# Linear attention and a SiLU feed-forward in one kernel: sums of x, sums of W2 and the first transposes of batch 1 placed elsewhere in the order of work

## The chip, the cores and the metric

The kernel runs on one core of a Trainium2 chip. The metric is the device time of one execution in microseconds, the median of several runs.

## The reference

q, k and v have the shape 8 batches x 8 heads x 576 tokens x 64, all float32. Attention is the linear kind: a softmax of q over its 64 features, a softmax of k over the 576 tokens, then two small products. Its output, 4608 tokens by 512, is the x of a feed-forward layer with a hidden width of 2048.

```python
q_s = exp(q) / sum(exp(q), axis=-1)          # over the features
k_s = exp(k) / sum(exp(k), axis=2)           # over the tokens
kv  = einsum('bhsd,bhse->bhde', k_s, v)
x   = einsum('bhsd,bhde->bhse', q_s, kv)     # then (tokens, heads*64)
h   = x @ w_in                               # 4608 x 2048
out = (h * sigmoid(h)) @ w_out               # 4608 x 512
```

## The kernel before, in words

**Two layers of work.** A batch of attention gives 576 rows of x. The feed-forward part works on chunks of 512 tokens, nine in all. Chunk t needs the rows of batch t and some of the batch before, so batch t+1 is prepared while chunk t is multiplied.

**Preparing a batch.** q, k and v come in halves of four heads each (`load`, L97). ScalarE takes the exponential of q (`exp_q`, L108, into `eq`) and of k (`exp_k`, L113, into `ek`). The row sums of q's exponentials are taken either by VectorE alone (`qsum`, L148 to L152) or, for batch 1, by GpSimd in two pair additions (`qsum_pair`, L126 and L129, into h tiles) and then by VectorE (`qsum_end`, L136 and L137). `qnorm` (L157) multiplies `eq` by the reciprocal sums, on GpSimd or VectorE. v is cast into `vaug` (`vcast`, L91 or L89). Normalised q is transposed into `qT`: for later batches by a DMA transpose (L167), for batches 0 and 1 by TensorE (`tr`, L175, nine small transposes for a half) with copies out of PSUM (`trcopy`). `kv_both` multiplies k and v (L189) and scales the result (L200, L202, `kvn`); `xt` multiplies it with `qT` (L228) and copies x, transposed, into `XTS` (XT in the profile), half on VectorE and half on ScalarE.

**The two matrix products.** Both large products use a scheme that does a two-by-two block product with seven block products instead of eight, at the price of sums of the blocks. For x @ w_in the products are `group` (L368), with sums of W1's blocks in WS (`ws_op`, L319) and sums of x's blocks in XS (`xs_op`, L329), both on VectorE. XS2 is made from XS1, and XS4 from XS2. The order of the seven is 1, 2, 6, 5, 7, 4, 3; product 6 reads XS2. The results are copied (`group_snap`, L89, ScalarE or VectorE), added (`group_add`, L346, VectorE) and put through SiLU (`group_silu`, L352, ScalarE). For the product with w_out the block products are `prod` (L467), with sums of the hidden values in S (`s_op`, L441) and four sums of W2's blocks T1 to T4 (`t_op`, L451). T2 needs T1, T4 needs T2. T3 is written over a block of W2 itself (`T3 = B12`); T1 and the plain product of chunk 0 read that block before. The results leave over `snap` (L483) and `w_add` (L487) into `ow` and `store` (L401).

**The start is different.** The first 576 tokens go through `wide` (L258) with a tanh form of SiLU (L250, L251), chunk 0's second product is plain (`mm2_plain`, L405), and `mm2_plain_out` (L417 on ScalarE, L419 on VectorE) writes its four 128-row tiles. Eight units of chunk 1 are plain as well (`mm1`, L276 and L287).

**The order of the work is written by hand.** The program keeps a list of units, each some TensorE work, and for every unit a list of pieces that are emitted just before it (`plan(u, f)`). Every engine takes its instructions in the order of emission. Pieces of one unit are emitted in the order of the `plan` calls. Units 0 to 15 are `wide`; `b1 = begin[1] = 16` starts nine plain units of chunk 0's second product; units 25 to 38 interleave its rest with seven groups of chunk 1; 39 to 46 are the eight plain units of chunk 1; `begin[2] = 47` starts chunk 2, where groups of chunk 2 and products of chunk 1 take turns ("ggbgbgbgbbgbgb", g for a group, b for half a product). The sums of x of chunk t are planned at `begin[t]`. The pieces that bear on this case are these:

```python
plan(b1, lambda: (tr(1, 0, 0, 5, 6), tr(1, 0, 5, J, 7)))
...
plan(b1 + 22, lambda: t_op(1, nc.vector))
...
plan(b1 + 30, lambda: t_op(3, nc.vector))
```

**Queues of transfers.** GpSimd issues the weights and the first batches' loads, up to batch 2; SyncE's queue holds the stores and all later loads, in order of emission. Tiles of q, k and v exist twice each (`ld`, bufs=2), so a load waits until the exponential or cast of the tile two loads earlier is done.

Of the kernel before, what the change touches and what calls it, by code (L numbers as in the profile page):

```python
# [8 lines left out]
FP32 = mybir.dt.float32  # L9
BF16 = mybir.dt.bfloat16  # L10
FP16 = mybir.dt.float16
ACT = mybir.ActivationFunctionType
# [5 lines left out]
def kernel(  # L18
# [9 lines left out]
    nc = tc.nc  # L28
    B, H, S, D = q.shape
    DM, DFF = w_in.shape  # L30
    NT = B * S
    P = 64
    J = S // P
# [10 lines left out]
    OS = 0.5 / XS  # L44
# [9 lines left out]
    mp = ctx.enter_context(tc.tile_pool(name="mp", bufs=2))  # L54
# [19 lines left out]
    PS = ps.tile([128, 8, 512], FP32, name="PS")  # L74
# [10 lines left out]
    st = [dict() for _ in range(B)]  # L85

    def copy(eng, o, i):
        if eng is nc.scalar:
            eng.copy(out=o, in_=i)  # L89
        else:  # L90
            eng.tensor_copy(o, i)  # L91

    def load(b, name, src, cc, eng):
        t = ld.tile([128, 2, J * D], FP32, name=name)
        st[b][name, cc] = t
        x = src[b].rearrange("(g r) (p j) d -> g (r p) (j d)", r=2, j=J)
        eng.dma_start(out=t, in_=x.rearrange("g x y -> x g y")[:, 2 * cc:2 * cc + 2, :])  # L97

    def jgd(b, name, cc):
        return st[b][name, cc].rearrange("p g (j d) -> p j g d", d=D)  # L100

    def half(t, cc):
        return t[:, :, cc * 128:(cc + 1) * 128].rearrange("p j (g d) -> p j g d", d=D)

    def exp_q(b, cc, g0=0, g1=2):
        if "eq" not in st[b]:
            st[b]["eq"] = ap.tile([128, J, NG * D], BF16, name="eq")
        nc.scalar.activation(  # L108
            out=half(st[b]["eq"], cc)[:, :, g0:g1], in_=jgd(b, "qt", cc)[:, :, g0:g1], func=ACT.Exp
        )  # L110

    def exp_k(b, cc):
        nc.scalar.activation(out=half(ek, cc), in_=jgd(b, "kt", cc), func=ACT.Exp)  # L113
# [6 lines left out]
    def qsum_pair(b, cc):  # L120
        e = half(st[b]["eq"], cc)
        t1 = mp.tile([128, 2 * TCH], FP32, name="h0", bufs=1)[:, 0:J * D]
        t1 = t1.rearrange("p (j g d) -> p j g d", g=2, d=D // 2)
        t2 = mp.tile([128, 2 * TCH], FP32, name=f"h{cc + 1}", bufs=1)[:, 0:J * D // 2]
        t2 = t2.rearrange("p (j g d) -> p j g d", g=2, d=D // 4)
        nc.gpsimd.tensor_tensor(  # L126
            out=t1, in0=e[:, :, :, 0:D // 2], in1=e[:, :, :, D // 2:D], op=ALU.add
        )
        nc.gpsimd.tensor_tensor(  # L129
            out=t2, in0=t1[:, :, :, 0:D // 4], in1=t1[:, :, :, D // 4:D // 2], op=ALU.add  # L130
        )
        st[b]["t2", cc] = t2

    def qsum_end(b, cc):
        new_zq(b)
        nc.vector.reduce_sum(out=st[b]["zq"][:, cc], in_=st[b]["t2", cc], axis=AX.X)  # L136
        nc.vector.reciprocal(out=st[b]["rzq"][:, cc], in_=st[b]["zq"][:, cc])  # L137

    def new_zq(b):
        if "zq" not in st[b]:  # L140
            st[b]["zq"] = ap.tile([128, 2, J, 2], FP32, name="zq", bufs=2)
            st[b]["rzq"] = ap.tile([128, 2, J, 2], FP32, name="rzq", bufs=2)
# [11 lines left out]
    def qnorm(b, cc, eng):  # L154
        e = half(st[b]["eq"], cc)
        r = st[b]["rzq"][:, cc]
        eng.tensor_tensor(  # L157
            out=e, in0=e, in1=r[:, :, :, None].to_broadcast([128, J, 2, D]), op=ALU.mult
        )

    def new_qt(b):
        if "qT" not in st[b]:
            st[b]["qT"] = ap.tile([128, J, 2, 128], BF16, name="qT", bufs=2)
        return st[b]["qT"]
# [7 lines left out]
    def tr(b, cc, j0, j1, bank):  # L172
        t = PS[:, bank, :].bitcast(BF16)
        for j in range(j0, j1):
            nc.tensor.transpose(  # L175
                out=t[:, (j - j0) * 128:(j - j0 + 1) * 128],
                in_=st[b]["eq"][:, j, cc * 128:(cc + 1) * 128],
                identity=ident,
            )

    def trcopy(b, cc, j0, j1, bank, eng=nc.vector):
        t = PS[:, bank, :].bitcast(BF16)[:, 0:(j1 - j0) * 128].rearrange("x (j y) -> x j y", y=128)
        copy(eng, new_qt(b)[:, j0:j1, cc, :], t)
# [127 lines left out]
    def ws_op(i, g):  # L311
        w, f0, f1 = WS[g], 4 * g + 8, 4 * g
        in0, in1, op = {
            1: (wa(0, f1), wa(1, f1), ALU.add),
            2: (w[0], wa(0, f0), ALU.subtract),
            3: (wa(0, f0), wa(0, f1), ALU.subtract),
            4: (wa(1, f0), w[1], ALU.subtract),
        }[i]
        nc.vector.tensor_tensor(out=w[i - 1], in0=in0, in1=in1, op=op)  # L319
# [30 lines left out]
    def group_silu(t, i, f, n):  # L350
        x = group_bank(t, False) if i is None else four(t, i)
        nc.scalar.activation(out=group_out(t, f, n), in_=x, func=ACT.Silu, scale=1.0 / XS)  # L352
# [42 lines left out]
    def rows(t, col):  # L395
        b, c = divmod(t * TCH + col, S)
        return out[b * S:(b + 1) * S, :].rearrange("(p j) o -> j p o", j=J)[c // P]

    def store(t, col, o):
        for i in range(2):  # L400
            nc.sync.dma_start(out=rows(t, col + i * P), in_=o[i * P:(i + 1) * P, :])  # L401
# [8 lines left out]
                stop=(fc == NFB - 1),  # L410
            )

    def mm2_plain_out(t, ms):
        ow = mp.tile([128, 2, DM], FP32, name="ow", bufs=3)
        for i, m in enumerate(ms):
            if i == 0:
                nc.scalar.activation(out=ow[:, i], in_=PS[:, 2 + m], func=ACT.Copy, scale=OS)  # L417
            else:
                nc.vector.tensor_scalar_mul(out=ow[:, i], in0=PS[:, 2 + m], scalar1=OS)  # L419
            store(t, m * 128, ow[:, i])  # L420

# [19 lines left out]
    def t_op(i, eng, f0=0, f1=HF):  # L443
        o, in0, in1 = {
            1: (T1, B12, B11),
            2: (T2, B22, T1),
            3: (T3, B22, B12),
            4: (T4, B21, T2),
        }[i]
        f = slice(f0, f1)  # L450
        eng.tensor_tensor(out=o[:, f], in0=in0[:, f], in1=in1[:, f], op=ALU.subtract)  # L451
# [97 lines left out]
    def load_w2(f0, f1):  # L549
        nc.gpsimd.dma_start(  # L550
            out=W2[:, f0:f1, :],
            in_=w_out[f0 * 128:f1 * 128, :].rearrange("(fc p) o -> p fc o", p=128),
        )
# [58 lines left out]
    def plan(u, f):  # L612
        at.setdefault(u, []).append(f)
# [7 lines left out]
    begin = {1: len(units)}  # L621
# [133 lines left out]
    for i in (1, 2, 6, 5, 7, 4, 3):  # L755
# [3 lines left out]

    b1 = begin[1]  # L760

    plan(9, lambda: (load_w2(8, 12), exp_q(1, 0, 0, 1)))
    plan(10, lambda: (exp_q(1, 0, 1, 2), qsum_pair(1, 0)))
    plan(10, lambda: load(2, "qt", q, 0, nc.gpsimd))
    plan(12, lambda: (exp_q(1, 1, 0, 1), qsum_end(1, 0), qnorm(1, 0, nc.gpsimd)))
    plan(13, lambda: (exp_q(1, 1, 1, 2), qsum_pair(1, 1)))
    plan(14, lambda: load(2, "qt", q, 1, nc.gpsimd))
    plan(b1 + 1, lambda: exp_k(1, 0))
    plan(b1 + 2, lambda: exp_k(1, 1))
    plan(b1, lambda: (tr(1, 0, 0, 5, 6), tr(1, 0, 5, J, 7)))  # L770
    plan(b1, lambda: (trcopy(1, 0, 0, 5, 6, nc.scalar), trcopy(1, 0, 5, J, 7)))
    plan(b1, lambda: (qsum_end(1, 1), qnorm(1, 1, nc.vector)))
    plan(b1, lambda: load_w2(12, 16))
    plan(b1, lambda: nc.gpsimd.tensor_copy(GTS[1][:, :, 0:64], GTS[0][:, :, TCH:S]))
# [19 lines left out]
    plan(b1 + 17, lambda: exp_k(2, 1))  # L794
    plan(b1 + 17, lambda: (vcast(2, 0, nc.gpsimd), vcast(2, 1, nc.gpsimd)))
    plan(b1 + 22, lambda: (group_silu(1, 2, 4, 1), group_silu(1, 0, 12, 0)))
    plan(b1 + 22, lambda: t_op(1, nc.vector))
    plan(b1 + 23, lambda: mm2_plain_out(0, (0, 1)))
    plan(b1 + 24, lambda: group_silu(1, 1, 12, 1))
    plan(b1 + 24, lambda: (ws_op(1, 0), ws_op(2, 0)))  # L800
    plan(b1 + 24, lambda: [load(3, x, y, i, nc.sync) for x, y, i in (
        ("vt", v, 0), ("vt", v, 1), ("qt", q, 0), ("kt", k, 1), ("kt", k, 0), ("qt", q, 1)
    )])
    plan(b1 + 25, lambda: kv_both(2))
    plan(b1 + 26, lambda: t_op(2, nc.vector))
# [1 line left out]
    plan(b1 + 28, lambda: t_op(4, nc.vector))  # L807
    plan(b1 + 29, lambda: xt(2, 1))
    plan(b1 + 29, lambda: (ws_op(3, 0), ws_op(4, 0)))
    plan(b1 + 30, lambda: mm2_plain_out(0, (2, 3)))  # L810
    plan(b1 + 30, lambda: t_op(3, nc.vector))

    for u, f in enumerate(units):
        for g in at.get(u, ()):
# [33 lines left out]
```

The softmax here doesn't subtract the row's maximum and nothing guards it: scores larger than these inputs give would overflow.

## Time and profile before

The kernel takes 265.26 us (three runs, 264.96 to 265.47). The profiled span is 263.3 us.

| engine | busy, us | share of the span |
|---|---|---|
| TensorE, matmuls | 253.0 | 96% |
| TensorE, weight loads | 203.4 | 77% |
| VectorE | 208.6 | 79% |
| ScalarE | 186.7 | 71% |
| GpSimd | 66.3 | 25% |

The longest single waits of TensorE after the first microseconds of the kernel are these: 0.52 us at 32.5 us, where the first transposes of batch 1 wait for GpSimd's normalising, and 1.82 us at 67.7 us, where product 6 of chunk 2 waits for a sum of x. In the profile, PE is TensorE, PEld its weight loads, DVE VectorE, ACT ScalarE, POOL GpSimd and SP SyncE; a q after the name is the engine's sequencer. A timeline line gives the start in us, the duration in us, the engine, the line in the code, the operation, what it writes and reads with shapes, and how many were merged; the idle time before it and what ended it stand in brackets. W in a line that starts with L451 is T3, which lies in W2.

### The profile page before, as it was taken

How to read it: one execution, taken by the hardware profiler on the slowest of the kernel's cores; microseconds unless marked ns; L12 is line 12 of the kernel's file. 1: busy time of each engine (PE TensorE's matmuls, PEld its weight loads, DVE VectorE, ACT ScalarE, POOL GpSimd, SP SyncE). 2: the span in 40 equal slices, each digit the busy share in tenths (PEclk: the TensorE clock that was granted, in tenths of full speed). 3: DMA queues.
4: the chain of work that ended last, by engine and by line, in shares of the span. 5: the costliest groups of instructions: out<-in, count | busy, mean ns of one | idle time of the engine just before them, and what ended most of it. 6: DMA issues, size and time to landing. Idle time of an engine off the chain costs nothing.

```text
span 263.3 us, 6409 instructions
## 1 busy us (share of the span) xinstructions
PE 253.0 (96%) x2732; PEld 203.4 (77%) x2732; DVE 208.6 (79%) x268; ACT 186.7 (71%) x211; POOL 66.3 (25%) x63
## 2 busy tenths in 40 slices
PE   8899899999799999999999999999999999999993
PEld 3457645656688888888888888888888888888882
DVE  2867787679997999799979997999798448855932
ACT  5767875897696699669966996699664757574610
POOL 1753891632141305130513050305000000000004
PEclk9999999999999999999999999999999999999998
DMA  7999999679997489748974889650415002400534
GB/s 240 336 199 331 260 323 334 239 143 298 364 320 159 158 190 308 142 157 166 330 137 168 192 295 119 192 127 0 92 42 120 2 0 57 105 2 1 116 85 120
DMA packets 35452, 45.89 MB, mean 174 GB/s; under 512 B 16208, under 2 KB 19984, under 8 KB 35424
## 3 DMA queue, kind: packets, MB, share of 16 engines
q1 hardware_dynamic: 29488, 33.63, 47.2%
q0 software_dynamic: 5616, 11.60, 16.9%
q8 instruction: 21, 0.34, 0.5%
q10 hardware_dynamic: 320, 0.26, 0.3%
q14 instruction: 7, 0.06, 0.1%
HBM read 36.70 MB, written 9.44 MB: 175 GB/s over the span
## 4 chain that ended last, share of the span: by engine, by line
PE 77%; DVE 14%; POOL 2%; ACT 2%; issue 2%; DMA 1%; POOLq 0%; DVEq 0%; ACTq 0%
PE PS L467 33%; PE PS L368 31%; PE PS L405 5%; PE PS L258 3%; PE PS L228 2%; DVE zq L148 2%; DVE h L346 2%; PE PS L189 2%; DMA qt<-in_q_dram 1%; DVE T L451 1%; DVE eq L157 1%; DVE WS L319 1%; DVE S L441 1%; DVE GT L441 1%; DVE XS L329 1%
## 5 line engine op out<-in xcount | busy, mean ns | idle before, releaser
L346 DVE TENSOR_TENSOR h<-PS,h 128x1024 f32<-128x1024 f32 (+1 forms) x45 | 54.0, 1200 | 13.7 <-PE PS L368 7.8
L467 PEld LDWEIGHTS <-GT 128*128 128x128 f16 x512 | 49.6, 98 | 6.9 <-issue 1.2
L368 PEld LDWEIGHTS <-WS 128*128 128x128 f16 x480 | 46.8, 98 | 8.7 <-DVE XS L329 2.1
L467 PE MATMUL PS<-W,GT 128*128 128x256 f16 x384 | 49.1, 273 | 0.0
L368 PE MATMUL PS<-XS,WS 128*128 128x256 f16 (+1 forms) x360 | 46.3, 272 | 1.9 <-DVE XS L329 1.8
L352 ACT ACTIVATE GT<-h 128x1024 f16<-128x1024 f32 (+1 forms) x45 | 46.1, 1047 | 0.3 <-DVE h L346 0.3
L89 ACT COPY h<-PS 128x1024 f32<-128x1024 f32 (+1 forms) x35 | 35.1, 1003 | 12.9 <-PE PS L368 12.5
L157 POOL TENSOR_TENSOR eq<-eq,rzq 128x1152 bf16<-128x1152 bf16 x13 | 27.5, 2117 | 62.1 <-DVE rzq L152 61.8
L467 PEld LDWEIGHTS <-S 128*128 128x128 f16 x384 | 37.1, 98 | 5.4 <-issue 1.0
L368 PEld LDWEIGHTS <-W 128*128 128x128 f16 x360 | 34.7, 98 | 4.9 <-issue 0.5
L467 PE MATMUL PS<-T,S 128*128 128x256 f16 x256 | 32.7, 273 | 0.0
L368 PE MATMUL PS<-XT,W 128*128 128x256 f16 (+1 forms) x240 | 29.5, 272 | 0.1
L352 ACT ACTIVATE GT<-PS 128x1024 f16<-128x1024 f32 (+1 forms) x15 | 15.3, 1017 | 18.9 <-PE PS L368 18.9
L91 POOL CAST vaug<-vt 128x1152 bf16<-128x1152 f32 x12 | 13.9, 1166 | 42.6 <-DMA vt<-in_v_dram 42.6
L729 POOL DMA_DIRECT2D out_dram<-ow x5 | 2.7, 547 | 72.1 <-DVE ow L714 72.1
L108 ACT ACTIVATE eq<-qt 128x1152 bf16<-128x1152 f32 (+1 forms) x18 | 19.0, 1058 | 2.6 <-DMA qt<-in_q_dram 2.5
L113 ACT ACTIVATE ek<-kt 128x1152 bf16<-128x1152 f32 x16 | 18.4, 1154 | 1.3 <-DMA kt<-in_k_dram 1.3
L148 DVE TENSOR_REDUCE zq<-eq 128x18 f32<-128x1152 bf16 x12 | 16.1, 1345 | 3.9 <-ACT eq L108 3.9
L258 PE MATMUL PS<-XT,W 128*128 128x288 f16 x128 | 16.3, 286 | 0.5 <-DVE XT L91 0.2
L467 PE MATMUL PS<-W,S 128*128 128x256 f16 x128 | 16.5, 273 | 0.0
L487 DVE SCALAR_TENSOR_TENSOR ow<-PS,sc 128x512 f32<-128x512 f32 x7 | 4.8, 691 | 14.4 <-ACT sc L483 14.4
L258 PEld LDWEIGHTS <-W 128*128 128x128 f16 x128 | 12.4, 98 | 4.3 <-issue 1.3
(78 smaller groups left out, 348.4 us busy)
## 6 DMA issues: line engine op xcount, KB each, us to landing
out_dram<-ow SPq DMA_DIRECT2D x64, 128.0 KB, 2.4
qt<-in_q_dram SPq DMA_DIRECT2D x12, 576.0 KB, 5.0
kt<-in_k_dram SPq DMA_DIRECT2D x12, 576.0 KB, 5.5
vt<-in_v_dram SPq DMA_DIRECT2D x12, 576.0 KB, 5.2
qt<-in_q_dram POOLq DMA_DIRECT2D x4, 576.0 KB, 12.5
kt<-in_k_dram POOLq DMA_DIRECT2D x4, 576.0 KB, 12.4
vt<-in_v_dram POOLq DMA_DIRECT2D x4, 576.0 KB, 12.6
W<-in_moe_w_out_dram POOLq DMA_DIRECT2D x4, 512.0 KB, 15.4
```

The costliest lines, as they stand in the source:

```text
L89: eng.copy(out=o, in_=i)
L91: eng.tensor_copy(o, i)
L108: nc.scalar.activation(out=half(st[b]["eq"], cc)[:, :, g0:g1], in_=jgd(b, "qt", cc)[:, :, g0:g1], func=ACT.Exp)
L113: nc.scalar.activation(out=half(ek, cc), in_=jgd(b, "kt", cc), func=ACT.Exp)
L148: nc.vector.reduce_sum(out=z, in_=e, axis=AX.X)
L157: eng.tensor_tensor(out=e, in0=e, in1=r[:, :, :, None].to_broadcast([128, J, 2, D]), op=ALU.mult)
L258: nc.tensor.matmul(out=PS[:, 2 * (fb % 3) + n, 0:S // 2], lhsT=W1[:, c, fb * 128:(fb + 1) * 128], rhs=XTS[0][:, c, n * (S // 2):(n + 1) * ...
L346: nc.vector.tensor_tensor(out=four(t, i), in0=group_bank(t, True), in1=four(t, i), op=ALU.add)
L352: nc.scalar.activation(out=group_out(t, f, n), in_=x, func=ACT.Silu, scale=1.0 / XS)
L368: nc.tensor.matmul(out=PS[:, bank + p // 2, (p % 2) * HT:(p % 2) * HT + width(t)], lhsT=a[:, c, p * 128:(p + 1) * 128], rhs=bb[:, c, 0:wid ...
L405: nc.tensor.matmul(out=PS[:, 2 + tb, :], lhsT=GTS[t % 2][:, fc, tb * 128:(tb + 1) * 128], rhs=W2[:, fc, :], start=(fc == 0), stop=(fc == N ...
L467: nc.tensor.matmul(out=PS[:, bank, m * HN:(m + 1) * HN], lhsT=a[:, fc, m * 128:(m + 1) * 128], rhs=bb[:, fc, :], start=(first and fc == 0) ...
```

## The change

Three things are moved, and a few pieces around them.

- **T3 behind the sums of x of chunk 2.** `t_op(3)` goes from unit 46 to unit 48, so VectorE meets XS1 to XS4 first.
- **T1 into chunk 1.** `t_op(1)` goes from unit 38 to unit 34, between two additions of chunk 1's groups.
- **The first transposes of batch 1 one unit on**, from ahead of unit 16 to ahead of unit 17, with their copies; both exponentials of k of batch 1 are put behind them.

With these, the exponential of q, half 0, of batch 1 becomes one instruction in place of two, with its pair sums one unit earlier; batch 2's first load of q goes from unit 10 to unit 12, behind GpSimd's normalising of batch 1's half 0; `mm2_plain_out` takes one tile per call, and the load of batch 3's q half 0 and k half 1 are put between the stores of chunk 0's first two tiles, ahead of v. The purpose is that no product waits for a sum that could have been made before, and that loads come in the order of their need.

```diff
-    def mm2_plain_out(t, ms):
-        ow = mp.tile([128, 2, DM], FP32, name="ow", bufs=3)
-        for i, m in enumerate(ms):
...
+    def mm2_plain_out(t, m, eng):
+        if m % 2 == 0:
+            st[t]["ow"] = mp.tile([128, 2, DM], FP32, name="ow", bufs=3)
+        o = st[t]["ow"][:, m % 2]
...
-    plan(9, lambda: (load_w2(8, 12), exp_q(1, 0, 0, 1)))
-    plan(10, lambda: (exp_q(1, 0, 1, 2), qsum_pair(1, 0)))
-    plan(10, lambda: load(2, "qt", q, 0, nc.gpsimd))
+    plan(9, lambda: (load_w2(8, 12), exp_q(1, 0), qsum_pair(1, 0)))
     plan(12, lambda: (exp_q(1, 1, 0, 1), qsum_end(1, 0), qnorm(1, 0, nc.gpsimd)))
+    plan(12, lambda: load(2, "qt", q, 0, nc.gpsimd))
     plan(13, lambda: (exp_q(1, 1, 1, 2), qsum_pair(1, 1)))
     plan(14, lambda: load(2, "qt", q, 1, nc.gpsimd))
-    plan(b1 + 1, lambda: exp_k(1, 0))
-    plan(b1 + 2, lambda: exp_k(1, 1))
-    plan(b1, lambda: (tr(1, 0, 0, 5, 6), tr(1, 0, 5, J, 7)))
-    plan(b1, lambda: (trcopy(1, 0, 0, 5, 6, nc.scalar), trcopy(1, 0, 5, J, 7)))
+    plan(b1 + 2, lambda: (exp_k(1, 0), exp_k(1, 1)))
+    plan(b1 + 1, lambda: (tr(1, 0, 0, 5, 6), tr(1, 0, 5, J, 7)))
+    plan(b1 + 1, lambda: (trcopy(1, 0, 0, 5, 6, nc.scalar), trcopy(1, 0, 5, J, 7)))
     plan(b1, lambda: (qsum_end(1, 1), qnorm(1, 1, nc.vector)))
...
-    plan(b1 + 22, lambda: t_op(1, nc.vector))
-    plan(b1 + 23, lambda: mm2_plain_out(0, (0, 1)))
+    plan(b1 + 18, lambda: t_op(1, nc.vector))
+    plan(b1 + 23, lambda: mm2_plain_out(0, 0, nc.scalar))
+    plan(b1 + 23, lambda: (load(3, "qt", q, 0, nc.sync), load(3, "kt", k, 1, nc.sync)))
+    plan(b1 + 23, lambda: mm2_plain_out(0, 1, nc.vector))
...
     plan(b1 + 24, lambda: [load(3, x, y, i, nc.sync) for x, y, i in (
-        ("vt", v, 0), ("vt", v, 1), ("qt", q, 0), ("kt", k, 1), ("kt", k, 0), ("qt", q, 1)
+        ("vt", v, 0), ("vt", v, 1), ("kt", k, 0), ("qt", q, 1)
     )])
...
-    plan(b1 + 30, lambda: mm2_plain_out(0, (2, 3)))
-    plan(b1 + 30, lambda: t_op(3, nc.vector))
+    plan(b1 + 30, lambda: mm2_plain_out(0, 2, nc.scalar))
+    plan(b1 + 30, lambda: mm2_plain_out(0, 3, nc.vector))
+    plan(begin[2] + 1, lambda: t_op(3, nc.vector))
```

More of the change, by code (lines that the diff above doesn't have):

```diff
@@ L411, in mm2_plain @@
             )
-    def mm2_plain_out(t, ms):
-        ow = mp.tile([128, 2, DM], FP32, name="ow", bufs=3)
-        for i, m in enumerate(ms):
[L416 to L420, printed above, removed]
+    def mm2_plain_out(t, m, eng):
+        if m % 2 == 0:
+            st[t]["ow"] = mp.tile([128, 2, DM], FP32, name="ow", bufs=3)
+        o = st[t]["ow"][:, m % 2]
+        if eng is nc.scalar:
+            nc.scalar.activation(out=o, in_=PS[:, 2 + m], func=ACT.Copy, scale=OS)
+        else:
+            nc.vector.tensor_scalar_mul(out=o, in0=PS[:, 2 + m], scalar1=OS)
+        store(t, m * 128, o)
     WG = [dict() for _ in range(NCH)]
```

## The prediction

> **What bounds the kernel now.** I read first the busy line of each engine and the chain that ended last, then the engines' busy time by stretches, then the waits and the timeline of the two stretches that the edits touch.
>
> ```profile
> PE 253.0 (96%) x2732; PEld 203.4 (77%) x2732; DVE 208.6 (79%) x268; ACT 186.7 (71%) x211; POOL 66.3 (25%) x63
> ...
> PE 77%; DVE 14%; POOL 2%; ACT 2%; issue 2%; DMA 1%; POOLq 0%; DVEq 0%; ACTq 0%
> ```
>
> TensorE carries the end, and 14% of the chain runs over VectorE. The stretches say where (the first column after the time is the length, then TensorE's busy time, the weight loads', VectorE's):
>
> ```profile
> 54.13:68.22 14.09, 11.91 (x153) 7.10 (x152) 13.92 (x20) 9.68 (x17) 3.19 (x3) 1.00 0.96 272
> 68.22:83.00 14.78, 14.74 (x198) 12.61 (x197) 14.57 (x18) 14.36 (x15) 4.24 (x2) 1.00 0.87 276
> ```
>
> From 54 to 83 us VectorE never rests; from 54 to 68 TensorE loses 2.2 us, and from 68 to 83 both are full. After 83 us the chain is TensorE alone. So microseconds that TensorE gains before 83 us should come off the end one for one. The hole and what makes it (idle time before an instruction stands in brackets):
>
> ```profile
> 54.13 1.09 DVE L346 TENSOR_TENSOR h<-PS,h 128x896 f32<-128x896 f32 x1 [2.09 <-PE PS L368]
> 55.14 1.22 DVE L451 TENSOR_TENSOR T<-W 128x2048 f16<-128x2048 f16 x1
> ...
> 63.57 1.16 POOL L91 CAST vaug<-vt 128x1152 bf16<-128x1152 f32 x1 [8.65 <-DMA vt<-in_v_dram]
> ...
> 64.02 1.79 DVE L451 TENSOR_TENSOR W<-W 128x2048 f16<-128x2048 f16 x1
> ...
> 65.60 1.23 POOL L91 CAST vaug<-vt 128x1152 bf16<-128x1152 f32 x1 [0.86 <-DMA vt<-in_v_dram]
> 65.73 1.37 DVE L329 TENSOR_TENSOR XS<-XT 128x512 f16<-128x512 f16 x1
> ...
> 67.68 1.05 PE L368 MATMUL PS<-XS,WS 128*128 128x256 f16 x8 [1.82 <-DVE XS L329]
> ...
> 68.06 1.28 ACT L108 ACT_TABLE_LOAD   x1 [2.83 <-DMA qt<-in_q_dram]
> 68.22 1.22 DVE L346 TENSOR_TENSOR h<-PS,h 128x1024 f32<-128x1024 f32 x1
> ```
>
> Product 6 of chunk 2 needs XS2, the second sum of x. It stands behind T3 (64.02). VectorE had idled 2.09 us before 54.13 and then did T1. The early stretch:
>
> ```profile
> 30.35 2.11 POOL L157 TENSOR_TENSOR eq<-eq,rzq 128x1152 bf16<-128x1152 bf16 x1 [0.28 <-DVE rzq L137]
> ...
> 32.43 1.27 POOL L126 TENSOR_TENSOR h<-eq 128x576 f32<-128x576 bf16 x1
> ...
> 32.52 0.68 PE L175 MATMUL PS<-ident,eq 128*128 128x128 bf16 x9 [0.52 <-POOL eq L157]
> ...
> 35.40 1.54 DVE L157 TENSOR_TENSOR eq<-eq,rzq 128x1152 bf16<-128x1152 bf16 x1
> ```
>
> TensorE waits 0.52 us for GpSimd's normalising of batch 1, half 0; the second transposes start at 37.35, 0.4 us after VectorE's normalising of half 1 ends.
>
> **What the Trainium skill says.** "SBUF — State Buffer", Who interferes with whom: a VectorE instruction with two SBUF inputs and a GpSimd instruction that reads SBUF exclude one another; the second waits for the whole first. The trace agrees: T3 took 1.79 us across a GpSimd cast where T1, of the same shape, took 1.22, and XS1 took 1.37 across the next cast where its later siblings took 0.42. "Perfetto Trace Analysis", GPSIMD Engine Instruction: GpSimd's durations are to be taken from start to start; 30.35 to 32.43 gives 2.08, near the printed 2.11. "DMA: Bandwidth & Descriptors", Issuing engines are not separate DMA queues: all issues share the same 16 engines. Here the share is 0.96 in the first stretch above, so a load put earlier makes another later.
>
> **The change part by part.**
>
> *T1 from unit 39 to unit 34.* On VectorE it comes to lie between the addition that starts at 50.95 (1.09 long, so to 52.04) and the one at 54.13. It costs 1.13 from start to start (55.14 to 56.27) and fits in the 2.09 hole, if the port is free. But GpSimd normalises from 50.60 to 52.72 and then casts twice, 52.67 to 54.93. T1 waits to 52.7; if it then takes the port ahead of the casts, it ends at 53.9, in time, and the casts slip by 1.1 to about 56.1, just before batch 2's kv products want them at 56.4. If the casts go first, T1 runs from 53.8 or 54.9 and nothing is gained. I take the first: gain 1.13 on VectorE's queue, low end 0.
>
> *XS1 to XS4 ahead of T3.* T3 and XS1 to XS2 were stretched by the two casts: 0.57 plus 0.95. With T1 gone I walk VectorE's queue from 54.13: addition to 55.2, ow to 55.8, two sums of W1 to about 57.5 (a slipped cast may hold them 0.4), kv's copy to 58.2, T2 to 59.3, XT copy to 60.4, T4 to 61.5, two sums of W1 to 62.7, ow to 63.3, XS1 and XS2 to 64.0, XS4 at 64.7, T3 to 65.85, then the addition for group 2, which began at 68.22. So it begins 2.3 to 2.6 us earlier. TensorE's own path from 54.79: matmuls of 0.75 per unit, kv 0.73, two xt of 0.34; its small holes at 58.95 and 61.22 (about 0.3 and 0.4) close and it reaches product 6 at about 64.9 against 67.68. XS2 is there. The next product of the other bank waits for the addition that is now behind T3, to 67.0: 0.1 to 0.3 lost. Since VectorE is full to 83 us, the gain there is VectorE's: 2.3 to 2.6.
>
> *Loads of batch 3 reordered, ow split.* The two ow writes are as before (0.59 and 0.68). q and k come before the second store and before v. q was issued at 60.16 and let ScalarE wait 2.83 us, to 68.06; it is now issued at about 57.6 and should land near 63. Without it the exponentials would bar the gain, as ScalarE's snapshot "sa" (71.48) stands behind them. But all six loads of 0.59 MB share the engines: 3.5 MB at the 385 to 400 GB/s that the trace moves from 65 to 71 us is 9 us, so the last land near 71 as before. v0 and v1 land at about 66 and 68, and their casts then fall on T3 or on S1 and S2 (up to 1.1 us each; before they cost 1.5). k half 0 lands near 70, and ScalarE wants it at 68.4: its snapshot of group 7 behind it may come 1 us late. I take 0.7 of loss for these together, ends 0 and 1.3.
>
> *First transposes one unit on, exponentials joined.* One exponential of 1.17 in place of two of 0.68 with a tanh between ends at 26.5, not 27.2, so the pair sums on GpSimd are ready before VectorE comes to them (it had waited 0.24), and GpSimd normalises from about 30.1 to 32.2. The first transposes now follow four matmuls (0.87 us) and start at 32.8 without a wait: 0.5 gained there. But batch 2's q load, 0.72 of GpSimd's time and formerly issued at 29.35 while GpSimd waited, is now queued between that normalising and the pair sums of half 1. These start at 32.9 against 32.43, and VectorE's normalising of half 1 ends at 37.4 against 36.94. The second transposes wait for that to about 37.45 against 37.35. The hole has moved by 5 us, not closed. Behind it on VectorE stand two sums of W1, half of a cast of v and a transpose copy, which kv's second half and xt wait for: 0.5 later, of which slack of 0.25 hides half. I take a loss of 0.25, ends -0.3 (if the load costs GpSimd nothing) and +0.5.
>
> Sum: 2.6 gained on VectorE's queue, less 0.7 for casts and loads, less 0.25 early: 1.65. **265.26 - 1.65 = 263.6 us.**
>
> **The rivals.** *Everything fits*: the casts miss the sums, the early part is neutral: 2.6 off, 262.7. For it: T1's hole is wide enough. Against: VectorE's queue has no idle time to dodge the casts. *T1 doesn't fit*: the casts on GpSimd go first; the queue is as before up to 64.0, less T3 ahead of XS: 1.7 less 0.7 less 0.25, some 0.75 off, 264.5. For it: the back-to-back GpSimd work from 50.60. *Gain eaten*: ScalarE waits for k half 0 and bars group 4, and the early loss is 0.5: about 265.2. *Slower*: the early wait for half 1 grows past 0.5 and pushes the chain kv, xt, XT copy to group 2 (already waiting at 44.15) by 1 us, and T1 delays the addition at 54.13 so that kv waits for its bank; XS gains only what these lose: 265.9. For it: five VectorE instructions queue behind that normalising; against: the hole of 1.82 us at 67.68 has one plain cause, which goes.
>
> **How the numbers follow.** Forecast 0.52, everything fits 0.15, T1 doesn't fit 0.16, gain eaten 0.09, slower 0.08. The range from 262.5 to 264.9 holds the first three with the ends of the costs: loads and casts from 0 to 1.3, early from -0.3 to +0.5. 0.2% is 0.53 us, so faster is below 264.73: the first three cases less a little, 0.80; same 0.12; slower 0.08.
>
> **What would show it.** Product 6 of chunk 2 without a wait for XS; T1 starting between 52 and 53 us and T3 directly after XS4; GpSimd's casts of v half 0 and 1 after 65 us with a stretched VectorE sum beside them; no wait of ScalarE for q of batch 3; a wait of the first transposes of 0 and of the second for VectorE's normalising of 0.3 to 0.7 us. The forecast is wrong if ScalarE comes to stand for a load at 68 to 71 us, if T1 starts after 54, or if TensorE's stretch after 83 us is not simply moved.

## The result, and the profile after

The changed kernel takes 264.19 us (four runs, 263.92 to 264.40) beside 265.37 us of the kernel before on the same chip (four runs, 264.96 to 265.74): 1.18 us less, a ratio of 0.9955 with a 95% interval from 0.9938 to 0.9973. The forecast was 263.6 us, 1.65 less. The profiled span went from 263.3 to 262.4 us. The two profiled executions took 265.12 and 264.17 us. In the table of the experiments below, the ratio and its interval come from the single runs and not from the two medians, so that the two can differ by 0.1%. From `t_op` on, the lines of the changed code have numbers higher by one: T sums are L452, products of the second layer L468, S sums L442.

First the stretches that answer to those shown of before (length, then busy time of TensorE, its weight loads, VectorE, ScalarE, GpSimd):

```profile
54.13:68.22 14.09, 13.97 (x175) 8.90 (x173) 13.38 (x21) 12.88 (x19) 2.72 (x3) 1.00 0.93 275
68.22:83.00 14.78, 13.87 (x191) 11.90 (x189) 14.57 (x16) 11.84 (x13) 6.73 (x4) 1.00 0.86 287
```

TensorE now works 13.97 of the first 14.09 us, where it had 11.91. In the second stretch it works 13.87 of 14.78, where it had 14.74. So a part of what was gained before 68 us was lost after it. The timeline of the changed kernel shows both:

```profile
52.48 1.85 DVE L452 TENSOR_TENSOR T<-W 128x2048 f16<-128x2048 f16 x1
...
53.19 3.26 POOL L91 CAST vaug<-vt 128x1152 bf16<-128x1152 f32 x2
...
54.65 1.09 DVE L346 TENSOR_TENSOR h<-PS,h 128x896 f32<-128x896 f32 x1 [0.33 <-PE PS L368]
...
64.34 0.42 DVE L329 TENSOR_TENSOR XS<-XT,XS 128x512 f16<-128x512 f16 x1
...
65.35 1.22 DVE L452 TENSOR_TENSOR W<-W 128x2048 f16<-128x2048 f16 x1
65.73 1.04 PE L368 MATMUL PS<-XS,WS 128*128 128x256 f16 x8
66.49 1.22 DVE L346 TENSOR_TENSOR h<-PS,h 128x1024 f32<-128x1024 f32 x1
...
69.33 1.74 POOL L91 CAST vaug<-vt 128x1152 bf16<-128x1152 f32 x1 [0.35 <-DMA vt<-in_v_dram]
...
70.14 1.99 DVE L442 TENSOR_TENSOR S<-S,GT 128x2048 f16<-128x2048 f16 x1
...
70.69 1.16 ACT L113 ACTIVATE ek<-kt 128x1152 bf16<-128x1152 f32 x1 [1.43 <-DMA kt<-in_k_dram]
...
72.19 1.05 PE L468 MATMUL PS<-T,S 128*128 128x256 f16 x8 [0.78 <-DVE S L442]
```

T1 stands in the old hole at 52.48, and the hole before the addition has shrunk from 2.09 to 0.33 us. XS2 takes 0.42 us, T3 1.22 without a stretch, and product 6 of chunk 2 starts without a wait at 65.73. The new wait is at 72.19: product 6 of chunk 1 waits for S2, which took 1.99 us, where it had taken 1.23, because it stood beside a cast on GpSimd (69.33 above). The same two steps in the kernel before:

```profile
71.80 1.23 DVE L441 TENSOR_TENSOR S<-S,GT 128x2048 f16<-128x2048 f16 x1
...
73.08 1.05 PE L467 MATMUL PS<-T,S 128*128 128x256 f16 x8
```

And the early stretch, where the hole has moved:

```profile
32.34 0.74 POOL L97 DMA_DIRECT2D qt<-in_q_dram  x1
32.50 1.04 PE L405 MATMUL PS<-W,GT 128*128 128x512 f16 x4 [0.22 <-DMA W<-in_moe_w_out_dram]
...
33.10 1.29 POOL L126 TENSOR_TENSOR h<-eq 128x576 f32<-128x576 bf16 x1
33.37 0.67 PE L175 MATMUL PS<-ident,eq 128*128 128x128 bf16 x9
...
36.09 1.54 DVE L157 TENSOR_TENSOR eq<-eq,rzq 128x1152 bf16<-128x1152 bf16 x1
...
37.78 0.66 PE L175 MATMUL PS<-ident,eq 128*128 128x128 bf16 x9 [0.29 <-ACT vaug L89]
```

The first transposes no longer wait, but the load at 32.34 pushes the pair sums from 32.43 to 33.10, and VectorE's normalising starts at 36.09 in place of 35.40. The waits list names ScalarE's cast as the last release of the second transposes; VectorE's normalising ends at 37.63, and the transposes start 0.15 after that. They read what it wrote, so it is the cause; the run of the early part alone, below, names it.

Start times of the same TensorE work in both kernels give the account:

| TensorE work | before, us | after, us | difference |
|---|---|---|---|
| second transposes of batch 1 | 37.35 | 37.78 | +0.43 |
| groups 1 and 2 of chunk 1 | 43.08 | 43.61 | +0.53 |
| groups 1 and 2 of chunk 2 | 63.08 | 63.11 | +0.03 |
| group product 6 of chunk 2 | 67.68 | 65.73 | -1.95 |
| group product 5 of chunk 2 | 69.49 | 67.76 | -1.73 |
| product 6 of chunk 1 | 73.08 | 72.19 | -0.89 |
| last matmuls of the kernel | 257.00 | 256.10 | -0.90 |

So 0.53 is lost early, 2.48 is gained between chunk 1's first groups and product 6 of chunk 2, 1.06 is given back by 73 us, and nothing more happens to the end. These are single traces. In the seven that have the changed early part as it is (this one and six of the runs below), groups 1 and 2 of chunk 1 start between 43.39 and 43.87 us; in the three with the early part of before, between 42.96 and 43.36. A difference of 0.2 us between two traces at this point means little, and the early loss is better taken as some 0.4 us.

### The profile page after: what moved, and what is told of

Its sections match the earlier page's. It is cut to its first block, busy times and chain, and to the rows that moved or that the text cites. A ratio compares the mean times of both kernels' runs of the same rounds, so it can differ in the third digit from the quotient of the medians.

```text
span 262.4 us, 6406 instructions
## 1 busy us (share of the span) xinstructions
PE 252.6 (96%) x2732; PEld 203.2 (77%) x2732; DVE 208.3 (79%) x268; ACT 186.7 (71%) x210; POOL 67.8 (26%) x63
## 4 chain that ended last, share of the span: by engine, by line
PE 73%; DVE 9%; DMA 9%; issue 4%; ACT 2%; POOL 1%; POOLq 0%; DVEq 0%; ACTq 0%
PE PS L468 33%; PE PS L368 31%; DMA W<-in_moe_w_out_dram 6%; PE PS L405 4%; DMA W<-in_moe_w_in_dram 3%; PE PS L228 2%; PE PS L189 2%; DVE h L346 2%; DVE S L442 1%; DVE zq L148 1%; DVE GT L442 1%; DVE T L452 1%; ACT ek L113 1%; POOL out_dram L730 1%; PE PS L276 1%
## 5 line engine op out<-in xcount | busy, mean ns | idle before, releaser
L468 PEld LDWEIGHTS <-GT 128*128 128x128 f16 x512 | 49.6, 98 | 6.9 <-issue 1.2
L468 PE MATMUL PS<-W,GT 128*128 128x256 f16 x384 | 49.1, 273 | 0.0
L468 PEld LDWEIGHTS <-S 128*128 128x128 f16 x384 | 37.1, 98 | 6.3 <-DVE S L442 1.1
L368 PEld LDWEIGHTS <-W 128*128 128x128 f16 x360 | 34.7, 98 | 4.8 <-issue 0.5
L468 PE MATMUL PS<-T,S 128*128 128x256 f16 x256 | 32.7, 273 | 0.8 <-DVE S L442 0.8
L91 POOL CAST vaug<-vt 128x1152 bf16<-128x1152 f32 x12 | 15.4, 1291 | 46.4 <-DMA vt<-in_v_dram 30.3
L468 PE MATMUL PS<-W,S 128*128 128x256 f16 x128 | 16.5, 273 | 0.0
L251 DVE SCALAR_TENSOR_TENSOR GT<-sg,PS 128x576 f16<-128x576 f32 x16 | 11.8, 752 | 5.3 <-ACT sg L250 5.1
```

The costliest lines, as they stand in the source:

```text
L251: nc.vector.scalar_tensor_tensor(out=o, in0=s, scalar=1.0, in1=i, op0=ALU.add, op1=ALU.mult)
L368: nc.tensor.matmul(out=PS[:, bank + p // 2, (p % 2) * HT:(p % 2) * HT + width(t)], lhsT=a[:, c, p * 128:(p + 1) * 128], rhs=bb[:, c, 0:wid ...
L468: nc.tensor.matmul(out=PS[:, bank, m * HN:(m + 1) * HN], lhsT=a[:, fc, m * 128:(m + 1) * 128], rhs=bb[:, fc, :], start=(first and fc == 0) ...
```

## The experiments

**My theory** was that the early part costs because of one load on GpSimd's queue, that the gain comes from VectorE's queue between 54 and 68 us, and that a cast beside S2 gives part of it back. **The rival** was that the early part is neutral or a gain and that loads and ScalarE make the shortfall. Every time below is a median; the kernel before ran beside each, and the difference is to that. The intervals are 0.6 to 1.2 us wide, so the times alone don't part two kernels that are 0.3 us from one another; there only the traces speak.

| kernel | time, us | before, us | difference | ratio, 95% interval |
|---|---|---|---|---|
| whole change | 264.19 | 265.37 | -1.18 | 0.9955, 0.9938 to 0.9973 |
| early part alone | 265.51 | 265.15 | +0.36 | 1.0013, 1.0001 to 1.0025 |
| late part alone | 263.56 | 265.15 | -1.59 | 0.9944, 0.9924 to 0.9964 |
| q load later | 263.69 | 265.15 | -1.46 | 0.9944, 0.9923 to 0.9965 |
| v last | 263.18 | 265.15 | -1.97 | 0.9919, 0.9901 to 0.9936 |
| T1 put back | 264.77 | 265.11 | -0.34 | 0.9995, 0.9979 to 1.0011 |
| T3 put back | 264.11 | 265.11 | -1.00 | 0.9958, 0.9945 to 0.9972 |
| loads put back | 265.06 | 265.11 | -0.05 | 1.0002, 0.9989 to 1.0014 |
| no casts of batch 3 | 263.70 | 265.11 | -1.41 | 0.9950, 0.9936 to 0.9964 |
| both mends | 262.75 | 265.11 | -2.36 | 0.9903, 0.9880 to 0.9926 |
| both mends, T3 behind | 263.64 | 265.11 | -1.47 | 0.9944, 0.9927 to 0.9961 |
| the same, early part as before | 263.79 | 265.11 | -1.32 | 0.9956, 0.9938 to 0.9973 |
| both mends, two sums early | 262.70 | 265.13 | -2.43 | 0.9909, 0.9888 to 0.9931 |

**Early part alone.** To the kernel before, only these lines of the change, in place of those that they replace there:

```diff
+    plan(9, lambda: (load_w2(8, 12), exp_q(1, 0), qsum_pair(1, 0)))
     plan(12, lambda: (exp_q(1, 1, 0, 1), qsum_end(1, 0), qnorm(1, 0, nc.gpsimd)))
+    plan(12, lambda: load(2, "qt", q, 0, nc.gpsimd))
...
+    plan(b1 + 2, lambda: (exp_k(1, 0), exp_k(1, 1)))
+    plan(b1 + 1, lambda: (tr(1, 0, 0, 5, 6), tr(1, 0, 5, J, 7)))
+    plan(b1 + 1, lambda: (trcopy(1, 0, 0, 5, 6, nc.scalar), trcopy(1, 0, 5, J, 7)))
```

> Only the early part of the change (first transposes a unit on, joined exponential, q load of batch 2 behind GpSimd's normalising); T1, T3, ow and the loads of batch 3 as before. My theory: the early part costs. The second transposes start at about 37.8 us in place of 37.35, kv of batch 1 at about 40.1 in place of 39.7; part of the 0.5 us is then swallowed by the wait for XS2 or not at all, so the time is 0.2 to 0.6 us above before. Rival (the early part is neutral or a gain, the shortfall lies wholly at 68 to 73 us): 0 to 0.4 us below before.

```profile
37.72 0.66 PE L175 MATMUL PS<-ident,eq 128*128 128x128 bf16 x9 [0.44 <-DVE eq L157]
```

It is 0.36 us slower, and the interval lies just above 1. The second transposes start at 37.72 with a wait of 0.44 us for VectorE's normalising, kv at 40.04, groups 1 and 2 of chunk 1 at 43.55. The hole at XS2 did not swallow the loss; it was 1.89 us, as wide as before.

**Late part alone.** To the changed kernel, the early lines as they were.

> The early part as before; T1, T3, ow and the loads of batch 3 as changed. My theory: product 6 of chunk 2 starts near 65.6 us, the wait for S2 stays at 0.8 to 0.9 us, and the time is 1.2 to 1.7 us below before, 0.1 to 0.5 below the whole change. Rival (early neutral): as the whole change, 0.9 to 1.2 below before.

It is 1.59 us faster than before. Together with the +0.36 of the early part that gives -1.23, and the whole change has -1.18: within the noise the two parts add. Product 6 of chunk 2 starts at 65.08, and the wait for S2 is there (0.73).

**The q load behind the pair sums.**

```diff
-    plan(12, lambda: load(2, "qt", q, 0, nc.gpsimd))
     plan(13, lambda: (exp_q(1, 1, 1, 2), qsum_pair(1, 1)))
+    plan(13, lambda: load(2, "qt", q, 0, nc.gpsimd))
```

> The changed kernel with one load moved: batch 2's first load of q is issued by GpSimd after the pair sums of batch 1's half 1 and not before them. My theory: the early loss is this issue of 0.74 us on GpSimd's queue. The pair sums start near 32.4, VectorE's normalising of half 1 ends near 36.9, the second transposes start at 37.3 to 37.4 without a wait, and the time falls by 0.3 to 0.6 us against the whole change. Rival (the early loss comes from the joined exponential, which made TensorE wait at 28.2 us, 0.3 us, and from the transpose copy that VectorE now does after its normalising): the second transposes move, but kv and the time fall by less than 0.2 us.

```profile
32.19 1.28 POOL L126 TENSOR_TENSOR h<-eq 128x576 f32<-128x576 bf16 x1
...
34.30 1.47 POOL L97 DMA_DIRECT2D qt<-in_q_dram  x2
...
37.12 0.66 PE L175 MATMUL PS<-ident,eq 128*128 128x128 bf16 x9
```

With the load gone from its place the pair sums start at 32.19, VectorE's normalising at 35.17, and the second transposes at 37.12 without a wait; groups 1 and 2 of chunk 1 start at 42.95 (whole change: 43.61). The load is the cause of the late second transposes. The time falls by 0.28 us more than the whole change's by the differences to before, just under what I expected, and by 0.50 by the times themselves; the intervals overlap, so the time alone doesn't show this gain. In the trace a part of the 0.66 us at chunk 1's groups is lost again, because S2 still waits for the second cast, which came only 0.49 us earlier (68.84 against 69.33): the wait of product 6 of chunk 1 grew from 0.78 to 0.95.

**v of batch 3 loaded last.**

```diff
-        ("vt", v, 0), ("vt", v, 1), ("kt", k, 0), ("qt", q, 1)
+        ("kt", k, 0), ("qt", q, 1), ("vt", v, 0), ("vt", v, 1)
```

> The changed kernel with the loads of batch 3 in the order q half 0, k half 1, k half 0, q half 1, v, v. My theory: GpSimd's casts of v at 67.8 and 69.3 us held S1 and S2 and so product 6 of chunk 1 by 0.8 us. With v last the casts start after 71 us, S2 takes 1.2 us and not 2.0, ScalarE's wait for k half 0 (1.43 us) goes too, and the time falls by 0.6 to 1.0 us against the whole change. Rival (S2 is late because VectorE's queue is full, not because of the casts): S2 is late as before and the time is within 0.2 us of the whole change. A second rival: v comes too late for batch 3's kv near 77.5 us, and the time rises.

```profile
69.86 1.22 DVE L442 TENSOR_TENSOR S<-S,GT 128x2048 f16<-128x2048 f16 x1
...
70.92 1.18 POOL L91 CAST vaug<-vt 128x1152 bf16<-128x1152 f32 x1 [14.69 <-DMA vt<-in_v_dram]
...
71.14 1.05 PE L468 MATMUL PS<-T,S 128*128 128x256 f16 x8
```

S2 takes 1.22 us and the casts come behind it; ScalarE's wait for k half 0 is gone (its exponential starts at 68.95, 70.69 in the whole change). The kernel is 1.97 us faster than before, 0.79 more than the whole change. It doesn't yet tell the cast from the wait for k, since both went.

**No casts of batch 3.** This parts them. The kernel leaves the two casts out, so that batch 3's attention is computed with batch 2's v.

```diff
-            plan(u + (2, 11)[i], lambda i=i: vcast(b, i, nc.gpsimd))
+            if b != 3:
+                plan(u + (2, 11)[i], lambda i=i: vcast(b, i, nc.gpsimd))
```

> The changed kernel without the two casts of v for batch 3: batch 3's attention is left with batch 2's v. My theory: S2 takes 1.2 us and product 6 of chunk 1 no longer waits for it, which shows that the casts held it; but ScalarE still waits 1.4 us for k half 0, its copy of group 7 still ends near 72.7 us and group 4 waits for that, so the time falls by only 0.1 to 0.4 us. Rival (the casts are the only bar): the time falls by 0.8 us, as with v loaded last.

```profile
69.83 1.23 DVE L442 TENSOR_TENSOR S<-S,GT 128x2048 f16<-128x2048 f16 x1
...
70.64 1.16 ACT L113 ACTIVATE ek<-kt 128x1152 bf16<-128x1152 f32 x1 [1.62 <-DMA kt<-in_k_dram]
...
72.75 1.03 PE L368 MATMUL PS<-XS,W 128*128 128x256 f16 x8 [0.60 <-ACT h L89]
```

S2 is back at 1.23 us, so the cast held it. But group product 4 then waits 0.60 us for ScalarE's copy of group 7, which stands behind the exponential of k half 0 (a wait of 1.62 us for the load). The gain is 0.23 us, less than the intervals can tell from none, and not the 0.79 of v last. Two bars stood behind one another, and the order with v last takes away both.

**T1 put back to unit 38.**

```diff
-    plan(b1 + 18, lambda: t_op(1, nc.vector))
+    plan(b1 + 22, lambda: t_op(1, nc.vector))
```

> The changed kernel with T1 alone put back to unit 38. My theory: T1's 1.13 us comes back onto VectorE's full queue, the addition for group 2 of chunk 2 starts near 67.3 us in place of 66.5, product 5 of chunk 2 waits for it, S1 and S2 come later by as much, and the time rises by 0.5 to 1.0 us against the whole change. Rival (T1 is the same work wherever it stands, and the casts set S2 anyway): within 0.2 us of the whole change.

0.84 us of the change's gain go by the medians against the kernel before, 0.58 by the times themselves, and the last matmuls start 0.50 later in the trace (256.60). The addition for group 2 starts at 67.06 in place of 66.49, group product 5 at 68.33 in place of 67.76, product 6 of chunk 1 at 72.69 in place of 72.19.

**T3 put back ahead of the sums of x.**

```diff
-    plan(begin[2] + 1, lambda: t_op(3, nc.vector))
+    plan(b1 + 30, lambda: t_op(3, nc.vector))
```

> The changed kernel with T3 alone put back ahead of the sums of x. My theory after the trace: T3 no longer meets the casts of v, which now come after 67 us, and VectorE is 0.5 us ahead; T3 takes 1.2 us from 63.8, XS2 is done near 65.9 and product 6 of chunk 2 waits 0.1 to 0.3 us; the addition that follows is no later. The time is 0 to 0.3 us above the whole change. Rival (the order of T3 and XS is what the change gains by, as its description and my prediction have it): product 6 waits over 0.8 us and the time rises by 0.6 us or more.

```profile
63.73 1.21 DVE L452 TENSOR_TENSOR W<-W 128x2048 f16<-128x2048 f16 x1
...
65.38 0.43 DVE L329 TENSOR_TENSOR XS<-XT,XS 128x512 f16<-128x512 f16 x1
...
65.86 1.05 PE L368 MATMUL PS<-XS,WS 128*128 128x256 f16 x8
66.39 1.22 DVE L346 TENSOR_TENSOR h<-PS,h 128x1024 f32<-128x1024 f32 x1
...
72.13 1.05 PE L468 MATMUL PS<-T,S 128*128 128x256 f16 x8 [0.81 <-DVE S L442]
```

264.11 us, a ratio of 0.9958 where the whole change has 0.9955: no difference that these intervals could show. Product 6 starts at 65.86, 1.10 after the product before it, so it lost some 0.2 us, and the addition behind is as early as ever. T3's place, the first item of the change, is worth nothing measurable once T1 and the casts are out of the way.

**Loads of batch 3 put back.** The two loads between the stores go, and the list is v, v, q half 0, k half 1, k half 0, q half 1 again.

> The changed kernel with batch 3's loads in the order and place of before (v, v, q half 0, k half 1, k half 0, q half 1, after both stores). My theory: casts of v near 63.5 and 65.6 us hold XS or T3 again by 1 us or more, ScalarE waits for q to about 68 us, its snapshot sa ends near 72 and holds product 6 of chunk 1; S2 itself takes 1.2 us. Two losses of 0.8 to 1 us stand in place of one: 0 to 0.6 us above the whole change. Rival (the order of loads does nothing): no difference in time, and ScalarE's exponential of q at the time of the whole change.

```profile
64.34 1.19 POOL L91 CAST vaug<-vt 128x1152 bf16<-128x1152 f32 x1 [7.63 <-DMA vt<-in_v_dram]
...
64.60 1.19 DVE L329 TENSOR_TENSOR XS<-XT,XS 128x512 f16<-128x512 f16 x1
...
66.05 1.37 DVE L329 TENSOR_TENSOR XS<-XT,XS 128x512 f16<-128x512 f16 x1
...
68.67 1.28 ACT L108 ACT_TABLE_LOAD   x1 [3.16 <-DMA kt<-in_k_dram]
...
69.74 1.03 PE L368 MATMUL PS<-XS,WS 128*128 128x256 f16 x8 [1.84 <-DVE h L346]
```

No gain is left: 265.06 us. The loss of the early part is in that, so by these medians T1 and the order of T3 and XS together still bring some 0.4 us. I had expected a loss of 0 to 0.6 against the whole change; it is 0.9 to 1.1. XS2 and XS4 are stretched by the two casts, from 0.42 to 1.19 and 1.37 us, the addition behind T3 comes at 68.48, and the hole of 1.8 us stands one group product later than before. The two stretches, 0.77 and 0.95, make 1.72 of the 1.98 us by which group product 5 comes later than in the whole change (69.74 against 67.76); the other 0.26 was there at chunk 1 already (groups 1 and 2 at 43.87 against 43.61). So ScalarE's wait of 3.16 us for its load has no part in this hole, and the casts make it. I had looked for the hold-up at XS and at product 6 of chunk 1, and had not seen that it falls on group product 5.

**Both mends together**, the q load later and v last.

> The changed kernel with both mends: batch 2's first q load behind the pair sums, and v of batch 3 loaded last. If the early loss and the loss at S2 are separate, the gains add: 0.4 to 0.5 for the first and 0.7 to 0.9 for the second, 2.3 to 2.6 us below before. Rival (the early gain is taken back at the next wait of VectorE's queue): as with v last alone, about 2.0 below before.

262.75 us, 2.36 below before. The sum of the parts is 1.18 + 0.28 + 0.79 = 2.25: within the noise they add. In this run the first matmuls of unit 16 waited 0.61 us for the load of W2 (0.22 in the whole change, none in the q load run). In the kernel before the transposes stand ahead of these matmuls, which then don't wait. Here the wait cost nothing that shows: groups 1 and 2 of chunk 1 start at 42.98, and at 42.95 in the q load run.

**T3 far behind, with both mends, and the same with the early part as before.**

```diff
-    plan(begin[2] + 1, lambda: t_op(3, nc.vector))
+    plan(begin[2] + 20, lambda: t_op(3, nc.vector))
```

> As the kernel with both mends, and T3 at unit 67, after S4, where VectorE idled 1.5 us near 83 us and before the product that reads it. If VectorE's full queue from 54 to 83 us is the bound that is left, its wait of 0.3 us at product 5 and of 0.2 us near 81 us go and the time is a further 0.3 to 0.6 us lower. Rival (TensorE is the bound everywhere by now): within 0.2 us of the kernel with both mends, or above it if T3 comes too late for its product.

> As the kernel with both mends and T3 late, but with the early part as it was before the change. If moving the first transposes brings anything once the q load is out of the way, this is 0.1 to 0.3 us slower than that kernel; if the early part is then neutral, the same within 0.1.

I placed T3 two units too far: the first half of product 7 comes before it, and so multiplies W2's own block in place of T3, and T3's write waits for that. The times are to be read with that change in the computation. T3 ends at 81.93 and the second half of product 7 waits 1.11 us for it. Up to there TensorE was ahead of the kernel with both mends (the group product before it at 79.83 against 80.61), so VectorE's queue was still a bound, but the kernel as a whole is 0.9 us slower. The two kernels differ by 0.15 us, less than the spread of their runs: whether the early part gains anything once the load is moved is not settled.

**Both mends, with T1 between XS1 and XS2 of chunk 1 and T2 in T1's place.**

```diff
-    plan(b1 + 10, lambda: (xs_op(1, 1), xs_op(1, 2), xs_op(1, 3), xs_op(1, 4)))
+    plan(b1 + 10, lambda: (xs_op(1, 1), t_op(1, nc.vector), xs_op(1, 2), xs_op(1, 3), xs_op(1, 4)))
...
-    plan(b1 + 18, lambda: t_op(1, nc.vector))
+    plan(b1 + 18, lambda: t_op(2, nc.vector))
...
-    plan(b1 + 26, lambda: t_op(2, nc.vector))
```

> The kernel with both mends (q load behind the pair sums, v of batch 3 last), and in it T1 between XS1 and XS2 of chunk 1, where VectorE idled 0.99 us, and T2 in T1's place. My theory: VectorE's full queue from 54 to 83 us is the bound that is left; with 1.13 us less in it product 5 of chunk 2 and product 3 near 80.6 us no longer wait (0.3 us each), and the time is 0.4 to 0.7 us below the kernel with both mends. Rival (TensorE's own sequence is the bound by now, or the second part of W2 lands too late for T2): within 0.2 us of it, or slower.

```profile
59.19 1.22 DVE L91 CAST XT<-PS 128x1024 f16<-128x1024 f32 x1 [1.12 <-PE PS L228]
...
67.20 1.03 PE L368 MATMUL PS<-XS,WS 128*128 128x256 f16 x8
```

262.70 us, the same as both mends alone, so my theory of this run fell. VectorE had 1.13 us less to do, and idled 1.12 us before the copy of XT at 59.19, because that waits for TensorE's product. From there the queue is what it was: group product 5 of chunk 2 starts at 67.20, with both mends alone at 67.13.

## Why the prediction was right, and where it was off

**What bounds the kernel: right.** What TensorE gained or lost before 83 us reached the end unchanged: -0.89 at 72 us and -0.90 at 256 us.

**T1: right.** It waited for GpSimd's normalising, took its turn ahead of the casts and ended at 54.33, 0.32 before the addition; the casts, stretched to 3.26 us for the two, slipped and hindered nobody. Putting it back cost 0.5 to 0.8 us, where I had 1.13 on the queue; some of it was taken up at the wait for S2, which the second cast set in both kernels. (The unit that T1 left is 38; the heading of that step says 39.)

**The sums of x ahead of T3: the size was nearly right, the credit was not.** The step had the addition for group 2 begin 2.3 to 2.6 us earlier. It began 1.73 earlier (66.49 for 68.22), and since VectorE came 0.52 late to the addition at 54.65, the queue gained 2.25 from there on. Product 6 came at 65.73 where the step had 64.9; 0.53 of that is the early loss, and the two small holes of TensorE ahead of it, which I put at 0.3 and 0.4 us, gave back 0.19 and 0.31 (start to start across each, 1.81 and 1.93 us before, 1.62 after). But the profile of before shows T3 ahead of XS2, and I spoke of the order as the cause of the hole. The run with T3 put back shows that the order does nothing measurable once the rest is changed. The gain lies in what my sum was made of, T1's 1.13 and the stretches by the casts (0.57 and 0.95), which I had counted but not followed to that end. The runs with one piece put back say the same: the loads, which move the casts, are worth 0.9 to 1.1 us, T1 0.5 to 0.8 and T3's place nothing, and the late part as a whole has 1.59.

**The loads: right in kind and nearly in size, the size in part by luck.** I put 0.7 us of loss on casts beside S1 and S2 and on k half 0, as a sum. The wait for S2 took back 0.84 (-1.73 to -0.89), the casts, expected from 66 and 68 us, began at 67.81 and 69.33, and k half 0, expected near 70, let ScalarE start at 70.69. The run without casts shows them as the cause of S2's delay, and that k half 0 stands as a second bar right behind it: the two hide one another and don't add. The Trainium skill ("SBUF — State Buffer", Who interferes with whom) has a VectorE instruction with two SBUF inputs and a GpSimd instruction that reads SBUF exclude one another, which agrees with these runs: S2 took 1.99 us beside a cast and 1.22 or 1.23 without.

**One of my signs of being wrong came true.** I had written that the forecast is wrong if ScalarE comes to stand for a load at 68 to 71 us. It did, 1.43 us for k half 0 up to 70.69. The time stayed in the range because the wait for S2 covered this one; with the casts gone it showed, as 0.60 us at group product 4.

**The early part: the mechanism was right, the size perhaps too small.** I took 0.25 us with an end of 0.5. The load on GpSimd's queue did what the step said, 0.2 to 0.3 us later at every point (pair sums 33.10 for 32.9, normalising's end 37.63 for 37.4, second transposes 37.78 for 37.45). The slack of 0.25 behind it hid nothing in this trace: groups 1 and 2 of chunk 1 were 0.53 late. Measured alone, the part costs 0.36 us, with an interval from 0.03 to 0.66 that holds the 0.25. TensorE also waited 0.40 us at 28.19 for a copy of the SiLU stretch and 0.22 at 32.50 for W2, neither of which the prediction had. They aren't the cause of the lateness: in the run of the early part alone they were 0.18 and nothing, and groups 1 and 2 came at 43.55 all the same.

The account of the traces is then 2.25 gained, less 0.84 at S2, less 0.52 early: 0.89, where the forecast had 2.6, 0.7 and 0.25. All three terms were off to the same side, and the range was wide enough for it. The medians show a gain of 1.18 us, 0.47 below the forecast, with an interval from 0.7 to 1.65, so how much of the shortfall is noise is open. Of the rivals, *everything fits* and *T1 doesn't fit* are ruled out by the trace. Both conditions of *gain eaten*, ScalarE's wait for k half 0 and an early loss of 0.5, are in the trace, but they took only a part of the gain.

## What to carry to other kernels

Where an engine's queue is full over a long stretch, ask which instructions in it are stretched by a neighbour before asking about their order: here the order of the loads decided which sums met GpSimd's casts, and it carried the larger part of the gain, while the swap of T3 and XS that the wait pointed to carried none that could be measured. A transfer issued from a queue that also computes is work in that queue; putting it one place on, in front of sums that others wait for, cost more than closing the hole of 0.52 us brought. And when a bar is taken away, look for the next one that ends at nearly the same time, as with the cast and k half 0.

## What the runs showed of the hardware

A load of q issued by GpSimd took 0.72 to 0.75 us of its queue and delayed what stood behind it by that much: from the start of the normalising to the pair sums it was 2.83 us with the load between (30.27 to 33.10) and 2.07 without (30.12 to 32.19).

A VectorE sum of two tensors in SBUF that was ready during a GpSimd operation ran, as far as the printed ends show, after it and ahead of GpSimd's next. T1 ended at 54.33, some 1.1 us after the end of the normalising that began at 51.13, and the casts behind then took 3.26 us for the two where they had taken 2.26. In the run of the late part alone it was the same: T1 1.85 us, the casts 3.25. I had taken this for the forecast and allowed for the opposite.
